# Linear attention and a gated MLP on one core: both heads of a pair of the recurrent state kept at the same columns

## The chip, the core and the metric

The kernel runs on one core of a Trainium2 chip. TensorE (PE) multiplies matrices, with its weight loads shown apart (PEld); VectorE (DVE), ScalarE (ACT) and GpSimd (POOL) work on elements; SyncE (SP) issues the DMAs. The metric is device microseconds of the whole program: 383.01 us before, the median of 3 runs (381.41 to 386.15).

## What is computed

Four batches, eight heads, 768 steps and 48 dimensions a head. Each head carries a 48 x 48 state that decays by a gate per dimension and takes up an outer product at each step; the output of a step is the query times the state:

```python
f = 1.0 / (1.0 + np.exp(-f_logit))
for t in range(S):
    state = f[:, :, t, :, None] * state + np.einsum('bhd,bhe->bhde', k[:, :, t], v[:, :, t])
    y[:, :, t] = np.einsum('bhd,bhde->bhe', q[:, :, t], state)
```

The heads side by side make x of 4 x 768 x 384. The second part is `h = relu(x @ w_in)` with 1024 columns, a 3-tap convolution of h along the sequence with a sigmoid behind it as a gate, and `(h * gate) @ w_out` back to 384 columns.

## The kernel before

The sequence of each batch is cut into 6 chunks of 128 steps; with 4 batches that makes 24 chunks, n = 0 to 23, with c the chunk's place in its batch. For each chunk:

- `stage_a` sums the logarithms of the gates along the chunk by a triangular matrix product (pl, L195), takes two exponentials of the sums (fi and fd, ScalarE) and scales the keys by fi (kp, L212) and the queries by fd (qp, L213, mostly on POOL). The decay over the whole chunk, one number per head and dimension, is put into `ft_all`, for the early chunks by small products, for the later ones by a DMA through DRAM.
- `stage_b` transposes keys and queries, two heads at a time: head j of pair p comes to partitions 64 j to 64 j + 47 (HP is 64, D is 48). The 16 partitions behind each head are zero, since the input's heads are padded to 64.
- `scores` makes 8 products of 48 x 128 by 48 x 128 (pa, L253), two halves of the array high, head j = 0 and head j = 1 into two banks of PSUM. VectorE masks them into am (L255).
- `state` makes 8 products keys by values (pk, L266) and updates the state (L273, or L276 and L277). The last chunk of a batch has no update.
- `values` makes the output in one bank, py: the state times the queries (L288, left out for the first chunk of a batch, except for the very first chunk, where the state is zero), and on top of it the masked scores times the values (L291). ScalarE rounds it into xT (L299) and VectorE stores the rest (L300); DMAs then bring together the parts of xT.

The state lies in two buffers st of 128 partitions, used in turn. For a pair of heads it is block diagonal: head 0 has partitions 0 to 47 and columns 0 to 47, head 1 partitions 64 to 111 and columns 64 to 111, and the rest was set to zero once. So one product of the whole array, 128 rows and 112 columns, serves both heads. The update goes head by head, since the columns differ: an add into tmp and a multiply by the decay, twice, with one buffer of tmp.

The MLP follows by half batches of 384 steps: `mm1` (ph, L328) with 9 products for each of 8 column blocks, each number split in two parts, then the convolution on ScalarE and VectorE (L333, L339, L340) and the gate (L342, L343); `mm2` splits the result (L358, L359) and makes the output (po, L365). The weights are split in two on ScalarE and VectorE during the first third of the program (tiles ms, L97 to L109).

The order is first set by a list: each piece of work has a due time in chunks (its chunk's number plus an offset), and the pieces are written in the order of these times. The framework's scheduler then arranges the instructions of all engines anew by its own estimate of durations and by which buffers are free. Each engine runs its instructions in its order. PSUM tiles pl, pt, pk share three buffers.

Of the kernel before, what the change touches and what calls it, by code (L numbers as in the profile page):

```python
# [9 lines left out]
F32 = mybir.dt.float32  # L10
# [5 lines left out]
ALU = mybir.AluOpType  # L16
PSUM = bass.MemoryType.PSUM
P = 128
# [4 lines left out]
CFG = dict(groups=[3, 3, 3, 3, 3, 3, 3, 3], sg=3, f1=2.6, g1=2.6, gv=2, gl=5.2, g=3.9, l=3.2, a=1.8, b=0.8, s=0.2, v=0.5, wil=(-2.3, -1.1), wis=(-0.7, 0.9), cw=1.3, wol=(1.3, 1.0), wos=2.1, wo=0.35, m1=0.5, m1s=0.9, m2=1.5, m2s=1.2, ek=(12, 24), ec='d', er='p', tp=0, tf=2, nw=2, gd=0, q0=2, lf=3, kpool=2, eg='d', eq='p', es='d', em='d', ew='p', xb=3, nf=6, fe='a', kb=4, qb=3, vb=4, lv=2.2, cb=1, sb=3, fi=1)  # L23

@with_exitstack
def gla_moe_kernel(ctx, tc, q_in, k_in, v_in, f_in, w_in, conv_w, w_out, out):


    nc = tc.nc
    B, S, H, D = v_in.shape  # L30
# [3 lines left out]
    NP = H // 2  # L34
# [9 lines left out]
    HP = 64  # L44
# [7 lines left out]
    wk = fast.enter_context(tc.tile_pool(name="wk", bufs=2))  # L52
# [17 lines left out]
    def zeroed(shape, n, name, eng):  # L70
        ts = [wk.tile(shape, F32, name=f"{name}{i}", bufs=1) for i in range(n)]
        for t in ts:
            eng.memset(t, 0.0)
        return ts
# [1 line left out]
    kp_b = [wk.tile([P, H, HP], F32, name=f"kp{i}", bufs=1) for i in range(CFG["kb"])]  # L76
    qp_b = [wk.tile([P, H, HP], F32, name=f"qp{i}", bufs=1) for i in range(CFG["qb"])]
    a_b = zeroed([P, 2, NP, P], 2, "am", nc.vector)
    s_b = zeroed([P, NP, HP + D], 2, "st", nc.vector)
    h_b = const.tile([P, NF, HS + 3], F32, name="hb")  # L80
    nc.gpsimd.memset(h_b[:, :, HS + 2:], 0.0)

    ft_all = const.tile([P, B, NC, NP], F32, name="ft_all")
# [173 lines left out]
    def state(n):  # L257
        b, c = steps[n]
        if c == NC - 1:
            return  # L260
        kp, kT, qT = tts[n]
        vt = qkv[n]
        pk = ps.tile([P, NP, D], F32, tag="s", name=f"pk{n}", bufs=3)
        for p in range(NP):
            for j in range(2):
                nc.tensor.matmul(pk[HP * j:HP * j + D, p, :], kp[:, 2 * p + j, :D], vt[:, 2 * p + j, :],  # L266
                                 start=True, stop=True)
        for j in range(2):
            r = slice(HP * j, HP * j + D)
            ft = ft_all[r, b, c, :].rearrange("p (n o) -> p n o", o=1).broadcast_to([D, NP, D])  # L270
            new = s_b[(n + 1) % 2][r, :, HP * j:HP * j + D]
            if c == 0:
                nc.vector.tensor_tensor(new, pk[r], ft, ALU.mult)  # L273
            else:
                tmp = wk.tile([P, NP, D], F32, tag="stmp", name=f"stmp{n}_{j}", bufs=1)
                nc.vector.tensor_tensor(tmp[r], pk[r], s_b[n % 2][r, :, HP * j:HP * j + D], ALU.add)  # L276
                (nc.vector if CFG["es"] == "d" else nc.gpsimd).tensor_tensor(new, tmp[r], ft, ALU.mult)  # L277

    def values(n):
        b, c = steps[n]  # L280
        kp, kT, qT = tts.pop(n)
        vt = qkv.pop(n)
        am = a_b[n % 2]
        py = ps.tile([P, NP, P], F32, tag="Y", name=f"py{n}")
        inter = c > 0 or n == 0
        if inter:
            for p in range(NP):
                nc.tensor.matmul(py[:HP + D, p, :], s_b[n % 2][:, p, :], qT[:, p, :], start=(p == 0), stop=False)  # L288
        for p in range(NP):
            for j in range(2):  # L290
                nc.tensor.matmul(py[HP * j:HP * j + D, p, :], vt[:, 2 * p + j, :], am[:, j, p, :],  # L291
                                 start=not inter and p == 0, stop=(p == NP - 1))
        hf = c // CPH
        if c % CPH == 0:
            xts[b, hf] = wk.tile([P, NP, 2, HS], F32R, tag="xT", name=f"xT{b}_{hf}", bufs=CFG["xb"])
        xT = xts[b, hf]
        ts = slice((c % CPH) * P, (c % CPH + 1) * P)
        for r in [slice(0, HP + D)] if c > 0 or n == 0 else [slice(0, D), slice(HP, HP + D)]:
            nc.scalar.copy(xT[r, :, 0, ts], py[r])  # L299
            nc.vector.tensor_tensor(xT[r, :, 1, ts], py[r], xT[r, :, 0, ts].bitcast(F32), ALU.subtract)  # L300
        if c % CPH == CPH - 1:
            for t in range(KT):
                for j in range(2):
                    s0, d0 = HP * j + GAP * t, HP * j + D
                    nc.sync.dma_start(xT[d0:d0 + GAP, t, :, :].bitcast(F32), xT[s0:s0 + GAP, KT, :, :].bitcast(F32))
# [89 lines left out]
    for n in range(N):  # L395
        plan(n - CFG["l"], lambda n=n: load_kq(n))
        plan(n - CFG["lv"], lambda n=n: load_v(n))
        plan(n - CFG["a"], lambda n=n: stage_a(n))
        plan(n - CFG["b"], lambda n=n: stage_b(n))
        plan(n - CFG["b"], lambda n=n: decay_out(n))  # L400
        plan(n - CFG["b"] + 0.4, lambda n=n: decay_in(n))
        plan(n, lambda n=n: scores(n))
        plan(n + CFG["s"], lambda n=n: state(n))
        plan(n + CFG["v"], lambda n=n: values(n))
# [29 lines left out]
    with tc.If(n_ok < P * n_ft):  # L434
        with ExitStack() as slow:
            wk = slow.enter_context(tc.tile_pool(name="swk", bufs=2))
# [11 lines left out]
            st = wk.tile([P, DG, D], F32, name="sst", bufs=1)  # L448
            nc.gpsimd.memset(st, 0.0)
            for t0 in range(0, S, TB):  # L450
# [31 lines left out]
                for t in range(0, TB, 8):  # L482
                    py = ps.tile([B * H, 8, D], F32, tag="sy", name=f"spy{t0}_{t}", bufs=2)
# [14 lines left out]
            for u in range(2 * B):  # L498
                b, hf = u // 2, u % 2
# [59 lines left out]
```

## Time and profile before

| | |
|---|---|
| median of 3 runs | 383.01 us (381.41 to 386.15) |
| the profiled execution | 384.77 us |
| its span, first to last instruction | 383.1 us |
| mean granted TensorE clock | 0.978 |
| busy: PE, PEld, DVE | 351.2, 313.2, 294.4 us |
| busy: ACT, POOL | 239.9, 60.1 us |
| chain that ended last, by engine | PE 60%, DVE 13%, ACT 9%, issue 5%, DMA 5%, POOL 3% |

A row of a group gives the line, engine, operation, output and inputs, shapes and count; behind the bar stand its busy time in us and the mean of one in ns, and then the idle time of the engine ahead of it. Matmuls are pipelined, so the mean of one is longer than the distance between two starts; the timeline, whose columns are the start in us, the length in us and the group, shows the distances. A row of a stretch gives its bounds and length in us, the busy time of each engine with the count of instructions, the granted clock, the DMA share and GB/s. A piece of the chain of waits gives its start and length in us, and engine, tile and line.

### The profile page before, as it was taken

What the parts mean: (1) busy time and instruction counts of PE and PEld (TensorE: products, weight loads), DVE (VectorE), ACT (ScalarE), POOL (GpSimd) and SP (SyncE); (2) the same over time, 40 slices, a digit from 0 to 9 for tenths busy, and PEclk for the clock granted to TensorE, in tenths of its full rate; (3) what the DMA queues carried; (4) which work ended last, traced back from release to release, by engine and by line L of the source; (5) the groups of instructions that cost most, each with busy time, mean ns of one, the idle gap of its engine ahead of it and who ended that gap; (6) DMA issues with size and microseconds to landing.
All of it is one profiled execution on the core that took longest, in us unless ns stands there. A gap on an engine that the chain in (4) does not pass through costs nothing.

```text
span 383.1 us, 7239 instructions
## 1 busy us (share of the span) xinstructions
PE 351.2 (92%) x2735; PEld 313.2 (82%) x2735; DVE 294.4 (77%) x467; ACT 239.9 (63%) x426; POOL 60.1 (16%) x72
## 2 busy tenths in 40 slices
PE   5578799868989699999999999999999999999993
PEld 1557578746978599989989999999989899999993
DVE  3999999988989968667688896669869776575620
ACT  3687669993997376645875665547545555566530
POOL 1111134311103701104011121204101100000000
PEclk9989999996999989999999999999999999999998
DMA  7999253324334330132313332232201000201011
GB/s 224 347 366 362 83 164 105 89 59 104 105 76 108 75 114 21 50 90 87 113 56 99 75 81 83 69 87 74 66 22 34 21 2 21 54 21 43 21 44 49
DMA packets 28854, 36.04 MB, mean 94 GB/s; under 512 B 10847, under 2 KB 20106, under 8 KB 28810
## 3 DMA queue, kind: packets, MB, share of 16 engines
q1 hardware_dynamic: 28810, 35.49, 31.0%
q8 instruction: 24, 0.39, 0.4%
q14 instruction: 20, 0.16, 0.2%
HBM read 28.37 MB, written 4.75 MB: 86 GB/s over the span
## 4 chain that ended last, share of the span: by engine, by line
PE 60%; DVE 13%; ACT 9%; issue 5%; DMA 5%; POOL 3%; SPq 2%; ACTq 0%; POOLq 0%; DVEq 0%
PE po L365 23%; PE ph L328 21%; PE pa L253 4%; PE py L291 4%; DMA fb<-in_f_logit_dram 4%; PE py L288 3%; POOL cgl L175 3%; PE ptk L235 2%; PE ptq L235 1%; PE pl L195 1%; ACT fb L169 1%; DVE g L340 1%; PE pk L266 1%; ACT g L342 1%; DVE am L255 1%
## 5 line engine op out<-in xcount | busy, mean ns | idle before, releaser
L328 PE MATMUL ph<-xT,wi 128*128 128x384 f32 x576 | 116.4, 349 | 4.8 <-ACT hb L331 2.7
L328 PEld LDWEIGHTS ph<-xT,wi 128*128 128x128 f32 x576 | 100.0, 189 | 10.4 <-issue 3.9
L365 PE MATMUL po<-wo,gh 128*128 128x384 f32 x384 | 101.3, 345 | 0.0
L365 PEld LDWEIGHTS po<-wo,gh 128*128 128x128 f32 x384 | 69.9, 191 | 1.2 <-issue 0.7
L365 PE MATMUL po<-wo,gl 128*128 128x384 f32 x192 | 65.8, 343 | 1.3 <-DVE gl L359 1.3
L339 DVE SCALAR_TENSOR_TENSOR g<-hb,cw,g 128x384 f32<-128x384 f32 (+1 forms) x64 | 41.0, 640 | 15.5 <-ACT g L333 15.1
L359 DVE TENSOR_TENSOR gl<-g,gh 128x1024 fp32r<-128x1024 f32 (+4 forms) x34 | 31.4, 934 | 27.1 <-ACT gh L358 27.0
L331 ACT ACTIVATE hb<-ph 128x384 f32<-128x384 f32 x64 | 31.3, 489 | 31.3 <-PE ph L328 31.2
L213 POOL TENSOR_TENSOR qp<-qp,fd 128x384 f32<-128x384 f32 x22 | 31.5, 1430 | 99.4 <-ACT fd L200 95.0
L340 DVE SCALAR_TENSOR_TENSOR g<-hb,cw,g 128x384 f32<-128x384 f32 (+1 forms) x64 | 44.2, 690 | 1.9
L343 DVE SCALAR_TENSOR_TENSOR g<-g,hb 128x768 f32<-128x768 f32 (+1 forms) x32 | 31.4, 981 | 14.6 <-ACT g L342 14.3
L342 ACT ACTIVATE g<-g 128x768 f32<-128x768 f32 (+1 forms) x32 | 27.1, 848 | 24.3 <-DVE g L340 24.3
L358 ACT CAST gh<-g 128x1024 fp32r<-128x1024 f32 (+4 forms) x34 | 26.5, 800 | 23.7 <-PE po L365 20.6
L333 ACT ACTIVATE g<-hb,cw 128x384 f32<-128x384 f32 (+1 forms) x64 | 39.6, 618 | 2.0
L365 PEld LDWEIGHTS po<-wo,gl 128*128 128x128 f32 x192 | 36.6, 191 | 1.7 <-DVE gl L359 1.5
L253 PE MATMUL pa<-qT,kT 48*128 48x128 f32 x384 | 32.8, 298 | 1.2 <-ACT qT L237 1.1
L253 PEld LDWEIGHTS pa<-qT,kT 48*128 48x128 f32 x384 | 26.1, 195 | 9.5 <-issue 5.5
L255 DVE COPY_PREDICATED am<-mask,pa 128x1024 f32<-128x1024 uint8 x24 | 31.4, 1309 | 1.2 <-PE pa L253 1.1
L291 PE MATMUL py<-am,v 128*48 128x128 f32 x384 | 27.4, 284 | 1.1 <-DVE am L255 0.9
L288 PE MATMUL py<-qT,st 128*112 128x128 f32 x168 | 24.1, 283 | 2.6 <-DVE xT L300 1.6
L291 PEld LDWEIGHTS py<-am,v 128*48 128x48 f32 x384 | 20.6, 126 | 6.1 <-DVE am L255 2.0
L299 ACT CAST xT<-py 112x512 fp32r<-112x512 f32 (+1 forms) x27 | 15.8, 585 | 15.0 <-PE py L291 11.6
(92 smaller groups left out, 428.5 us busy)
## 6 DMA issues: line engine op xcount, KB each, us to landing
kp<-in_k_dram SPq DMA_DIRECT2D x24, 256.0 KB
qp<-in_q_dram SPq DMA_DIRECT2D x24, 256.0 KB
fb<-in_f_logit_dram SPq DMA_DIRECT2D x24, 192.0 KB
v<-in_v_dram SPq DMA_DIRECT2D x24, 192.0 KB
out_dram<-ob SPq DMA_DIRECT2D x24, 192.0 KB
wis<-in_moe_w_in_dram SPq DMA_DIRECT2D x6, 512.0 KB
wos<-in_moe_w_out_dram SPq DMA_DIRECT2D x8, 384.0 KB
xT<-xT SPq DMA_DIRECT2D x48, 48.0 KB
```

Source lines behind the costliest of these rows:

```text
L213: (nc.vector if CFG["eq"] == "d" or n < CFG["q0"] else nc.gpsimd).tensor_tensor(qp[:, :, :D], qp[:, :, :D], fd, ALU.mult)
L253: nc.tensor.matmul(pa[:, j, p, :], kT[r, p, :], qT[r, p, :], start=True, stop=True)
L255: nc.vector.copy_predicated(am, mask, pa)
L288: nc.tensor.matmul(py[:HP + D, p, :], s_b[n % 2][:, p, :], qT[:, p, :], start=(p == 0), stop=False)
L291: nc.tensor.matmul(py[HP * j:HP * j + D, p, :], vt[:, 2 * p + j, :], am[:, j, p, :], start=not inter and p == 0, stop=(p == NP - 1))
L328: nc.tensor.matmul(ph, wi[:, t, wl, f * P:(f + 1) * P], xts[b, hf][:, t, xl, :], start=(i == 0), stop=(i == 3 * KT - 1))
L333: nc.scalar.activation(cv, hb[:, 1:n + 1], AF.Copy, scale=cw[:, 1, f:f + 1])
L339: nc.vector.scalar_tensor_tensor(cv, hb[:, 2:n + 2], cw[:, 2, f:f + 1], cv, ALU.mult, ALU.add)
L340: nc.vector.scalar_tensor_tensor(cv, hb[:, 0:n], cw[:, 0, f:f + 1], cv, ALU.mult, ALU.add)
L343: nc.vector.scalar_tensor_tensor(cv, cv, 1.0, h_b[:, fp:fp + 2, 1:n + 1], ALU.add, ALU.mult)
L359: nc.vector.tensor_tensor(lo, g[:, f:f + k], hi.bitcast(F32), ALU.subtract)
L365: nc.tensor.matmul(po, g[:, f, :], wo[:, f, wl, :], start=(i == 0), stop=(i == 3 * NF - 1))
```

## The change

The state is kept compactly: both heads of a pair at columns 0 to 47, head 0 on partitions 0 to 47, head 1 on 64 to 111, with 16 zero columns behind. The keys by values products are taken 64 wide, with the zero padding, so that pk is filled on all 128 partitions. Then the update is one add and one multiply over 128 partitions, with two buffers of tmp. The product of the state with the queries can no longer be one of the whole array, since the heads share columns; it becomes two of a quarter of the array each, rows and columns 0 to 63 for head 0, rows 64 to 127 and columns 64 to 111 for head 1. Nothing else is edited.

```diff
-    s_b = zeroed([P, NP, HP + D], 2, "st", nc.vector)
+    s_b = zeroed([P, NP, HP], 2, "st", nc.vector)
...
-                nc.tensor.matmul(pk[HP * j:HP * j + D, p, :], kp[:, 2 * p + j, :D], vt[:, 2 * p + j, :],
+                nc.tensor.matmul(pk[HP * j:HP * (j + 1), p, :], kp[:, 2 * p + j, :], vt[:, 2 * p + j, :],
                                  start=True, stop=True)
-        for j in range(2):
-            r = slice(HP * j, HP * j + D)
-            ft = ft_all[r, b, c, :].rearrange("p (n o) -> p n o", o=1).broadcast_to([D, NP, D])
-            new = s_b[(n + 1) % 2][r, :, HP * j:HP * j + D]
-            if c == 0:
-                nc.vector.tensor_tensor(new, pk[r], ft, ALU.mult)
-            else:
-                tmp = wk.tile([P, NP, D], F32, tag="stmp", name=f"stmp{n}_{j}", bufs=1)
-                nc.vector.tensor_tensor(tmp[r], pk[r], s_b[n % 2][r, :, HP * j:HP * j + D], ALU.add)
-                (nc.vector if CFG["es"] == "d" else nc.gpsimd).tensor_tensor(new, tmp[r], ft, ALU.mult)
+        ft = ft_all[:, b, c, :].rearrange("p (n o) -> p n o", o=1).broadcast_to([P, NP, D])
+        new = s_b[(n + 1) % 2][:, :, :D]
+        if c == 0:
+            nc.vector.tensor_tensor(new, pk, ft, ALU.mult)
+        else:
+            tmp = wk.tile([P, NP, D], F32, tag="stmp", name=f"stmp{n}", bufs=2)
+            nc.vector.tensor_tensor(tmp, pk, s_b[n % 2][:, :, :D], ALU.add)
+            nc.vector.tensor_tensor(new, tmp, ft, ALU.mult)
...
-                nc.tensor.matmul(py[:HP + D, p, :], s_b[n % 2][:, p, :], qT[:, p, :], start=(p == 0), stop=False)
+                for j in range(2):
+                    m = HP if j == 0 else D
+                    r = slice(HP * j, HP * j + D)
+                    nc.tensor.matmul(py[HP * j:HP * j + m, p, :], s_b[n % 2][r, p, :m], qT[r, p, :],
+                                     start=(p == 0), stop=False)
```

The scheduler makes a new order of all engines from this. On VectorE, before, the update of chunk 2 (pk_459 the keys by values, stmp_0 and stmp_1 the two heads' tmp, mswi and mscw the splitting of weights):

```order
L276 TENSOR_TENSOR stmp_0_468<-pk_459,st_95 48x192
L255 COPY_PREDICATED am_91<-mask_82,pa_438 128x1024
L98 TENSOR_SCALAR mscw<-mscw 24x128
L103 SCALAR_TENSOR_TENSOR mswi_1_338<-wis_148,mswi_1_338 128x512
L108 TENSOR_TENSOR mswi_1_338<-mswi_1_338,wi 128x512
L277 TENSOR_TENSOR st_96<-stmp_0_468,ft_all 48x4x48
L99 TENSOR_SCALAR mscw<-mscw 24x128
L109 TENSOR_TENSOR wi<-mswi_1_338 128x512
L276 TENSOR_TENSOR stmp_1_471<-pk_459,st_95 48x192
L300 TENSOR_TENSOR xT_0_294<-py_520,xT_0_294 112x4x128
L101 SCALAR_TENSOR_TENSOR mscw<-cws,mscw 24x128
L277 TENSOR_TENSOR st_96<-stmp_1_471,ft_all 48x4x48
```

After, the same update on VectorE (pk_463; the lines below the edit have other numbers, L302 is L300 of before):

```order
L274 TENSOR_TENSOR stmp_472<-pk_463,st_95 128x192
L212 TENSOR_TENSOR kp_87<-kp_87,fi_381 128x8x48
L109 TENSOR_TENSOR wi<-mswi_1_341 128x512
L302 TENSOR_TENSOR xT_0_297<-py_419,xT_0_297 112x4x128
L275 TENSOR_TENSOR st_96<-stmp_472,ft_all 128x4x48
```

Twelve places, four of them of the update, have become five with two of the update; the masking of this chunk's scores (L255) now stands behind the update instead of inside it.

On TensorE, before, around the state product of chunk 14 (py_2159; ptq the transposed queries, ph the MLP):

```order
L235 MATMUL ptk_2134<-ident,kp_87 128x128 x4
L235 MATMUL ptq_2141<-ident,qp_88 128x128 x4
L288 MATMUL py_2159<-qT_1974,st_95 112x128 x4
L291 MATMUL py_2159<-am_91,v_1768 48x128 x8
L328 MATMUL ph_6_2181<-xT_1_1429,wi 128x384 x5
```

After, the same chunk on TensorE (py_2174; L289 is the state product, L293 the values):

```order
L235 MATMUL ptq_2156<-ident,qp_88 128x128 x4
L289 MATMUL py_2174<-qT_1988,st_95 64x128
L289 MATMUL py_2174<-qT_1988,st_95 48x128
L289 MATMUL py_2174<-qT_1988,st_95 64x128
L289 MATMUL py_2174<-qT_1988,st_95 48x128
L289 MATMUL py_2174<-qT_1988,st_95 64x128
L289 MATMUL py_2174<-qT_1988,st_95 48x128
L289 MATMUL py_2174<-qT_1988,st_95 64x128
L289 MATMUL py_2174<-qT_1988,st_95 48x128
L293 MATMUL py_2174<-am_91,v_1786 48x128 x3
L195 MATMUL pl_2165<-cgh_1665,tri 128x384
```

Four products of 112 columns have become eight of 64 and 48 in turn, and the values of this chunk now have a gate sum in their midst. Over the whole order the pieces of consecutive state products are 30 instead of 26, since some are broken in the same way.

## The prediction

> **What bounds the kernel now.** I read the busy times of the whole execution first, then the engines by stretch, then the chain of waits.
>
> ```profile
> PE 351.2 (92%) x2735; PEld 313.2 (82%) x2735; DVE 294.4 (77%) x467; ACT 239.9 (63%) x426; POOL 60.1 (16%) x72
> ...
> 20.00:70.00 50.00, 43.61 (x447) 34.14 (x447) 49.32 (x95) 39.52 (x86) 13.63 (x7) 0.97 0.65 212
> 70.00:90.00 20.00, 13.50 (x116) 10.54 (x114) 18.86 (x35) 15.79 (x27) 4.87 (x6) 0.91 0.24 62
> 90.00:150.00 60.00, 55.34 (x434) 48.74 (x433) 51.86 (x85) 45.68 (x76) 12.77 (x11) 0.94 0.32 89
> 150.00:360.00 210.00, 209.81 (x1595) 195.58 (x1595) 157.49 (x228) 123.35 (x210) 26.03 (x33) 1.00 0.21 57
> ```
>
> The columns behind each stretch are its length, then PE, PEld, DVE, ACT and POOL busy. There are two regimes. From 20 to 70 us VectorE is busy 49.32 of 50 us and TensorE only 43.61. From 150 to 360 us TensorE is busy 209.81 of 210 and VectorE 157.49. So VectorE time counts early, and after 150 us only TensorE time does. Between 20 and 150 us TensorE idles 130 - 112.45 = 17.6 us: the most that a relief of other engines can give there. The chain agrees; its pieces include these:
>
> ```profile
> 37.93 1.05 DVE st L277
> ...
> 46.22 1.06 DVE st L277
> ...
> 52.96 4.08 DMA fb<-in_f_logit_dram
> ...
> 61.70 4.52 POOL cgl L175
> ...
> 84.53 3.45 DMA xT<-xT
> ...
> 116.11 1.08 DVE st L277
> ...
> 117.33 1.10 PE py L288 x8
> ```
>
> Three state multiplies are links of it, the last one shortly ahead of a state product; between 52 and 88 us its long links are a gate load, a POOL run and the xT copies.
>
> **VectorE: 72 instructions become 36.** Of 24 chunks 20 update the state; 4 of them (a batch's first) take 2 multiplies, 16 take 2 adds and 2 multiplies. After the change it is 1, or 1 and 1.
>
> ```profile
> L277 DVE TENSOR_TENSOR st<-stmp,ft_all 48x192 f32<-48x192 f32 x32 | 13.3, 415 | 0.6
> L276 DVE TENSOR_TENSOR stmp<-pk,st 48x192 f32<-48x192 f32 x32 | 11.2, 352 | 0.6
> ...
> L273 DVE TENSOR_TENSOR st<-pk,ft_all 48x192 f32<-48x192 f32 x8 | 2.8, 350 | 0.1
> ...
> L300 DVE TENSOR_TENSOR xT<-py,xT 112x512 fp32r<-112x512 f32 x21 | 14.4, 687 | 0.9 <-ACT xT L299 0.4
> ...
> L300 DVE TENSOR_TENSOR xT<-py,xT 48x512 fp32r<-48x512 f32 x6 | 4.1, 686 | 1.4 <-ACT xT L299 1.4
> ```
>
> No row has 128x192. The two forms of L300 answer that: 112 partitions take 687 ns, 48 take 686, so the number of partitions costs nothing, and I take 352 ns for each new add and multiply. Removed are 16 x 0.352 + 16 x 0.415 + 4 x 0.350 = 13.7 us. Where they lie:
>
> ```profile
> 20.00:70.00 50.00, 6.97 (x16) 0.97 0.65 212
> ...
> 90.00:150.00 60.00, 6.31 (x16) 0.94 0.32 89
> 150.00:360.00 210.00, 11.25 (x32) 1.00 0.21 57
> ```
>
> These are the adds and multiplies with tmp; the first-chunk multiplies stand apart:
>
> ```profile
> 20.00:70.00 50.00, 0.70 (x2) 0.97 0.65 212
> 70.00:90.00 20.00, 0.71 (x2) 0.91 0.24 62
> ```
>
> Half of 11.25 goes after 150 us, where TensorE hides it: worth nothing. Before that, half of 6.97, 6.31, 0.70 and 0.71 makes 7.3 us: the most that can reach the end, with 0 as the least.
>
> How much reaches the end? The multiplies of 1.05 us in the chain, three times the usual, stood beside POOL. Two of the cases:
>
> ```profile
> 37.63 1.13 POOL L213 TENSOR_TENSOR qp<-qp,fd 128x384 f32<-128x384 f32 x1 [6.24 <-ACT fd L200]
> 46.06 1.01 POOL L213 TENSOR_TENSOR qp<-qp,fd 128x384 f32<-128x384 f32 x1 [7.30 <-ACT fd L200]
> ```
>
> The multiply at 37.93 ends at 38.98, where POOL ends at 38.76; 46.22 ends at 47.28, POOL at 47.07. So a state multiply can wait out a POOL one; with half as many there will be fewer such hits. In 20 to 52 us lie one first-chunk update and three others, together 0.35 + 3 x 0.70 = 2.5 us saved, 3.9 if both long multiplies go as well (two times 0.7 more): I take 3.2. From 52 to 88 us the chain hangs on the load, POOL and the copies above, and I take nothing. From 88 to 150 us four updates save 2.8 to 3.5 us in a chain that they share with other work; I take 1.0, for the link at 116.11. VectorE gives -4.2 us (from 0 to -7.3).
>
> The state's path is shorter too. It was add, multiply, add, multiply with other work between, for chunk 1 from the row below to the end of the multiply at 37.93, 5.3 us; now it is one of each:
>
> ```profile
> 33.69 0.34 DVE L276 TENSOR_TENSOR stmp<-pk,st 48x192 f32<-48x192 f32 x1
> ```
>
> What waited for it, by the view of waits (us, times, longest):
>
> ```profile
> PE py L288 <- DVE st L277: 0.9, 2, 0.7
> ```
>
> 0.9 us in two waits; I leave them to the favourable end. The second tmp buffer is worth nothing (0.6 us idle ahead of all adds), nor are the smaller memsets, which stand at the program's start.
>
> **TensorE: 4 state products a chunk become 8 of a quarter array each.** 21 chunks have it.
>
> ```profile
> L288 PE MATMUL py<-qT,st 128*112 128x128 f32 x168 | 24.1, 283 | 2.6 <-DVE xT L300 1.6 <-DVE st L277 0.9
> ```
>
> A float32 product is two instructions (168 = 21 x 4 x 2), so 16 a chunk replace 8. The nearest rows are the other two tiled products, each 16 a chunk: scores in half-height tiles (L253), values in half-width tiles (L291).
>
> ```profile
> 244.67 1.04 PE L288 MATMUL py<-qT,st 128*112 128x128 f32 x8
> 245.63 1.08 PE L291 MATMUL py<-am,v 128*48 128x128 f32 x16
> 246.65 1.85 PE L328 MATMUL ph<-xT,wi 128*128 128x384 f32 x9
> 248.42 0.49 PE L253 MATMUL pa<-qT,kT 48*128 48x128 f32 x4
> 248.84 1.85 PE L328 MATMUL ph<-xT,wi 128*128 128x384 f32 x9
> 250.63 0.94 PE L253 MATMUL pa<-qT,kT 48*128 48x128 f32 x12
> 251.50 0.56 PE L266 MATMUL pk<-v,kp 128*48 128x48 f32 x16
> 251.99 0.65 PE L235 MATMUL ptk<-ident,kp 128*128 128x128 f32 x4
> ...
> 260.33 1.16 PE L253 MATMUL pa<-qT,kT 48*128 48x128 f32 x16
> 261.42 0.38 PE L266 MATMUL pk<-v,kp 128*48 128x48 f32 x8
> ```
>
> From start to next start, the 8 full products take 245.63 - 244.67 = 0.96 us, 16 values 1.02, 16 scores 1.09. So both kinds of half tile run in overlapping pairs, at twice the rate per instruction. If quarter tiles do so too, 16 cost between 1.02 and 1.09: +0.06 to +0.13 a chunk, 1.3 to 2.7 us over 21. Scores are the nearer row, since they too have 48 rows: +2.3, rounded down for the smaller weight load (48 or 64 columns, not 128). Breaking a group costs: 4 scores from 248.42 and 12 from 250.63 took 0.42 + 0.87 = 1.29 us against 1.09 for 16 in one piece, so 0.2 a break. The new order has 30 pieces of state product for 26, and a few more of values and scores, fewer of updates: I add 0.7. Update products load 64 columns, not 48; the 16 at 251.50 take 0.49, their loads hidden: 0, at most 0.1 a chunk, 2 us. TensorE costs +3.0 us (from 1.3 to 5).
>
> A gain on TensorE is excluded: at best both tiles of a pair run in the time of one full product.
>
> **Sum.** 3.0 - 4.2 = -1.2 us on the profiled 384.77 us (span 383.1), 383.6; that execution lies 1.8 above the median of 383.01, so 381.8, said as 382. The ends: -7.3 - 0.9 + 1.3 = -6.9, or 376, and +5, or 388.
>
> **Rivals.** *No overlap.* All diagonal tiles write one bank of py, and scores write two banks, one for each half. If the two quarter tiles cannot run at once, 16 instructions take the full tile's time each, 1.92 us a chunk for 0.96: 20 us over 21 chunks, of which these lie where nothing hides them:
>
> ```profile
> 150.00:360.00 210.00, 11.80 (x88) 10.98 (x88) 1.00 0.21 57
> ```
>
> 88 of the 168 instructions are 11 chunks, 10.6 us; so +10 to +20, 393 to 403. It decides once a chunk's product passes 0.96 + 7.7 / 21 = 1.33 us. For it: no row shows two row tiles in one bank. Against it: values put two column tiles in one bank (L291) and overlap, and the two halves here share no partition either. The Trainium skill, "TensorEngine Tiling (Array Packing)", Restrictions and Gotchas, says that different row tiles cannot access the same PSUM bank at the same time; by that rule this rival holds, and no run here shows it yet. 0.13.
>
> *Early relief in full.* All 7.3 us pass on, with the 0.9 us of waits and up to 1.0 us more (the excess of the long multiplies, 6.97 + 6.31 - 32 x 0.35 = 2.1 us, of which half is counted already), and quarter tiles are no slower than full ones: -8.2 to -9.2, 374 to 375. For it: VectorE at 99% there. Against: from 52 to 88 us the chain hangs on loads. 0.10.
>
> *The order slips.* The scheduler rebuilt the whole order. One gate piece put later costs a POOL run of this size on the chain:
>
> ```profile
> 123.67 6.25 POOL L175 TENSOR_TENSOR cgl<-fb,cgh 128x1152 fp32r<-128x1152 f32 x1 [1.32 <-ACT cgh L174]
> ```
>
> One or two such runs with part of the forecast gain lost are +5 to +10, 388 to 393. 0.10. That 128 partitions cost more than 48 is spoken against by L300.
>
> **How the numbers follow.** Forecast 382, its own range 376 to 388, 0.67. A difference of 2%, 7.7 us, is about what a measurement can tell. Faster by more is early relief, 0.10; slower by more is no overlap and half of the slip, 0.13 + 0.05 = 0.18; the rest, 0.72, is within 2%. The range 374.5 to 393 leaves out no overlap and the far half of early relief, 0.18.
>
> **What would show it.** State updates: 36 VectorE instructions near 0.35 us, VectorE near 281 us. State products: 336 instructions, 16 a chunk from start to next start in 1.0 to 1.1 us, with starts 0.06 apart; 0.1 apart, or 1.9 a chunk, is no overlap. TensorE still full from 150 us on, which may begin 2 to 5 us earlier. Wrong it would be if the new adds took well over 0.35 us, or TensorE's idle time before 150 us grew.

## The result, and the profile after

The changed kernel takes 387.0 us in the median of 20 runs (383.97 to 389.24), the kernel before 384.46 us beside it (20 runs, 381.41 to 387.53). The ratio is 1.0062, with a 95% interval of 1.004 to 1.0084: 2.4 us slower. That is within 2%, and within the range, but the sum had said 1.2 us faster.

First the busy times and the stretches of the profiled execution after (its own time 387.15 us, span 385.3); columns as before:

```profile
PE 360.5 (94%) x2903; PEld 315.3 (82%) x2903; DVE 282.2 (73%) x431; ACT 240.2 (62%) x426; POOL 51.6 (13%) x72
...
20.00:70.00 50.00, 46.48 (x472) 35.62 (x470) 46.38 (x86) 36.70 (x81) 10.09 (x7) 0.87 0.63 203
70.00:90.00 20.00, 13.29 (x116) 10.66 (x113) 17.73 (x33) 19.65 (x35) 1.72 (x3) 0.94 0.22 62
90.00:150.00 60.00, 60.00 (x492) 51.90 (x491) 50.97 (x79) 45.68 (x75) 11.08 (x13) 0.96 0.34 94
150.00:360.00 210.00, 210.00 (x1667) 191.13 (x1666) 148.89 (x205) 121.36 (x206) 25.89 (x33) 1.00 0.21 57
```

VectorE fell from 294.4 to 282.2 us. TensorE's idle time between 20 and 150 us fell from 17.6 to 130 - 119.8 = 10.2 us, and from 90 us on it is full. But its busy time rose by 9.3 us. The state's groups on VectorE:

```profile
L274 DVE TENSOR_TENSOR stmp<-pk,st 128x192 f32<-128x192 f32 x16 | 5.6, 351 | 2.5 <-PE pk L266 2.2
L275 DVE TENSOR_TENSOR st<-stmp,ft_all 128x192 f32<-128x192 f32 x16 | 5.6, 349 | 0.1
L271 DVE TENSOR_TENSOR st<-pk,ft_all 128x192 f32<-128x192 f32 x4 | 1.4, 349 | 0.0
```

36 instructions of 0.35 us, and none of them long: exactly what was costed. TensorE around the state product that stood at 244.67 us before, and one that is broken by a gate sum:

```profile
227.58 0.65 PE L289 MATMUL py<-qT,st 48*64 48x128 f32 x8
228.16 0.45 PE L195 MATMUL pl<-cgh,tri 128*128 128x384 f32 x1
228.44 0.34 PE L195 MATMUL pl<-cgl,tri 128*128 128x384 f32 x1
228.71 0.65 PE L289 MATMUL py<-qT,st 48*64 48x128 f32 x8
229.28 1.08 PE L293 MATMUL py<-am,v 128*48 128x128 f32 x16
...
244.46 1.09 PE L289 MATMUL py<-qT,st 48*64 48x128 f32 x16
245.47 1.08 PE L293 MATMUL py<-am,v 128*48 128x128 f32 x16
...
251.55 0.67 PE L266 MATMUL pk<-v,kp 128*64 128x48 f32 x16
252.16 0.66 PE L235 MATMUL ptk<-ident,kp 128*128 128x128 f32 x4
...
257.08 0.34 PE L195 MATMUL pl<-cgh,tri 128*128 128x384 f32 x1
257.25 0.34 PE L195 MATMUL pl<-cgl,tri 128*128 128x384 f32 x1
257.43 0.34 PE L367 MATMUL po<-wo,gl 128*128 128x384 f32 x1
```

Unbroken, the 16 quarter products take 1.01 us, 0.063 from start to start on average: the pairs overlap. Broken, they take 0.58 + 0.57 = 1.15, and the gate sum between the pieces 0.28 + 0.27, where one between output products, at 257.08, takes 0.17 + 0.18. The update products take 0.60 us, where they took 0.50 (the rows' starts are rounded, and give 0.61 and 0.49).

The groups from 150 us to the end, before:

```profile
L288 PE MATMUL py<-qT,st 128*112 128x128 f32 x88 | 11.8, 273 | 0.0
...
L266 PE MATMUL pk<-v,kp 128*48 128x48 f32 x160 | 6.7, 214 | 0.0
```

and after:

```profile
L289 PE MATMUL py<-qT,st 48*48 48x128 f32 (+1 forms) x176 | 13.2, 277 | 0.0
...
L266 PE MATMUL pk<-v,kp 128*64 128x48 f32 x160 | 7.9, 229 | 0.0
```

For the same number of chunks the state product has 1.4 us more and the update products 1.2. These are prices in a stretch where nothing hides them.

The two timelines can be laid side by side from the scores of chunk 13 to the last output product, with the same work between. Before:

```profile
178.34 1.16 PE L253 MATMUL pa<-qT,kT 48*128 48x128 f32 x16
...
376.82 0.34 PE L365 MATMUL po<-wo,gl 128*128 128x384 f32 x1
```

and after:

```profile
176.36 1.16 PE L253 MATMUL pa<-qT,kT 48*128 48x128 f32 x16
...
379.18 0.34 PE L367 MATMUL po<-wo,gl 128*128 128x384 f32 x1
```

The changed kernel comes to the first row 2.0 us earlier, and from there it takes 202.8 us instead of 198.5, 4.3 more: a gain early and a larger loss late.

### The profile page after: what moved, and what is told of

Same layout as the page of the kernel before. It is cut to its first block, busy times and chain, and to the rows that moved or that the text cites. A ratio compares the mean times of both kernels' runs of the same rounds, so it can differ in the third digit from the quotient of the medians.

```text
span 385.3 us, 7519 instructions
## 1 busy us (share of the span) xinstructions
PE 360.5 (94%) x2903; PEld 315.3 (82%) x2903; DVE 282.2 (73%) x431; ACT 240.2 (62%) x426; POOL 51.6 (13%) x72
## 4 chain that ended last, share of the span: by engine, by line
PE 78%; ACT 9%; DMA 4%; DVE 4%; SPq 1%; issue 1%; ACTq 0%; DVEq 0%
PE po L367 27%; PE ph L330 25%; PE pa L253 6%; PE py L293 6%; PE py L289 5%; PE pk L266 3%; PE ptk L235 3%; PE pl L195 2%; PE ptq L235 2%; DMA wis<-in_moe_w_in_dram 2%; ACT fb L169 1%; DMA fb<-in_f_logit_dram 1%; ACT g L335 1%; ACT fb L170 1%; DMA qp<-in_q_dram 1%
## 5 line engine op out<-in xcount | busy, mean ns | idle before, releaser
L367 PE MATMUL po<-wo,gh 128*128 128x384 f32 x384 | 100.1, 342 | 0.0
L341 DVE SCALAR_TENSOR_TENSOR g<-hb,cw,g 128x384 f32<-128x384 f32 (+1 forms) x64 | 39.7, 623 | 21.6 <-ACT g L335 21.5
L342 DVE SCALAR_TENSOR_TENSOR g<-hb,cw,g 128x384 f32<-128x384 f32 (+1 forms) x64 | 44.4, 695 | 1.9
L213 POOL TENSOR_TENSOR qp<-qp,fd 128x384 f32<-128x384 f32 x22 | 27.9, 1270 | 99.7 <-ACT fd L200 93.7
L253 PE MATMUL pa<-qT,kT 48*128 48x128 f32 x384 | 34.7, 304 | 1.6 <-ACT qT L237 1.6
L253 PEld LDWEIGHTS pa<-qT,kT 48*128 48x128 f32 x384 | 27.7, 201 | 9.9 <-issue 6.9
L255 DVE COPY_PREDICATED am<-mask,pa 128x1024 f32<-128x1024 uint8 x24 | 31.4, 1308 | 1.5 <-PE pa L253 1.5
L212 DVE TENSOR_TENSOR kp<-kp,fi 128x384 f32<-128x384 f32 x22 | 25.3, 1149 | 7.5 <-ACT fi L199 7.5
L293 PE MATMUL py<-am,v 128*48 128x128 f32 x384 | 30.1, 292 | 0.0
L289 PE MATMUL py<-qT,st 48*48 48x128 f32 (+1 forms) x336 | 27.5, 291 | 0.1
L293 PEld LDWEIGHTS py<-am,v 128*48 128x48 f32 x384 | 22.5, 130 | 5.8 <-issue 4.1
```

Source lines behind the costliest of these rows:

```text
L253: nc.tensor.matmul(pa[:, j, p, :], kT[r, p, :], qT[r, p, :], start=True, stop=True)
L255: nc.vector.copy_predicated(am, mask, pa)
L289: nc.tensor.matmul(py[HP * j:HP * j + m, p, :], s_b[n % 2][r, p, :m], qT[r, p, :], start=(p == 0), stop=False)
L341: nc.vector.scalar_tensor_tensor(cv, hb[:, 2:n + 2], cw[:, 2, f:f + 1], cv, ALU.mult, ALU.add)
L342: nc.vector.scalar_tensor_tensor(cv, hb[:, 0:n], cw[:, 0, f:f + 1], cv, ALU.mult, ALU.add)
L367: nc.tensor.matmul(po, g[:, f, :], wo[:, f, wl, :], start=(i == 0), stop=(i == 3 * NF - 1))
```

## Experiments

The theories that the expectations name: A, TensorE pays the prices just read, and VectorE's relief gives part of them back; B, the scheduler's new order decides; C and D, the price or the relief never reaches the end. All ratios are to the kernel before, run beside them.

**One part at a time, all chunks.** Two parts of the change, its relief without its price, and a second tmp buffer alone.

```diff
 e1: the state product alone, state block diagonal
-    py[:HP + D, p, :], s_b[n % 2][:, p, :], qT[:, p, :]
+    for j: py[HP * j:HP * j + m, p, :], s_b[n % 2][r, p, HP * j:HP * j + m], qT[r, p, :]
 e2: the update products alone
-    pk[HP * j:HP * j + D, p, :], kp[:, 2 * p + j, :D]
+    pk[HP * j:HP * (j + 1), p, :], kp[:, 2 * p + j, :]
 e3: one head's update
-    for j in range(2):
+    for j in range(1):
 e4: two buffers of tmp
-    name=f"stmp{n}_{j}", bufs=1
+    name=f"stmp{n}_{j}", bufs=2
```

> The kernel before with only its state product split into two quarter-array products a pair; the state stays block diagonal, the update stays two adds and two multiplies. Theory A (TensorE pays): in the profile after, 16 quarter products take 1.01 us with 0.1 us more ahead of them for the change of tile, against 0.96, so 0.05 to 0.15 us a chunk; 11 chunks lie in the full stretch and 10 in the early one, so +1.6 to +3.2 us, ratio 1.004 to 1.008. Theory B (the new order decides): no relation to that sum, between -3 and +3 us. Theory C (the loss is from elsewhere): 0, ratio 1.000.

> The kernel before with only the keys by values products taken 64 wide instead of 48. Theory A (TensorE pays): after the change 16 of them take 0.60 us against 0.49, so 0.11 us a chunk in 20 chunks; +1.1 us (the chunks of the full stretch alone) to +2.2 us, ratio 1.003 to 1.006, with 0.60 us for 16 in this profile too. The prediction's own term was 0. Theory B (order): its order differs little from before, so 0.

> The kernel before with the update of the second head of each pair left out (its state stays zero, so the odd heads miss what came from earlier chunks): VectorE has 36 state instructions fewer, as after the change, and TensorE the same products as before. Theory A: the early relief arrives, -2 to -4.2 us, ratio 0.989 to 0.995. Theory D (the relief never reaches the end, since loads and POOL hold the early stretch): 0, ratio 0.998 to 1.002. If A, TensorE's idle time before 150 us falls by as much.

> The kernel before with two buffers of tmp and nothing else: a small change of the order with no work added or removed. Theory A: within 1 us of before, ratio 0.998 to 1.002. Theory B (the order alone moves the time by as much as was measured): 2 us or more either way.

Measured: e1 0.997 (0.9944 to 0.9995), e2 0.9974 (0.9946 to 1.0002), e3 1.0103 (1.0052 to 1.0154), e4 1.0153 (1.011 to 1.0196). All four miss theory A: the prices came out as small gains (e2's interval reaches 1), the relief as a loss, and a change that adds and removes no work cost 1.5%, 5.9 us. The stretches of e4 show where:

```profile
20.00:70.00 50.00, 41.77 (x446) 32.87 (x444) 46.39 (x86) 35.27 (x80) 9.69 (x7) 0.97 0.64 212
70.00:90.00 20.00, 15.68 (x112) 13.81 (x112) 17.16 (x32) 18.70 (x31) 3.72 (x3) 0.83 0.21 53
90.00:150.00 60.00, 51.93 (x440) 46.84 (x439) 54.95 (x91) 43.67 (x72) 12.32 (x12) 0.91 0.35 98
150.00:360.00 210.00, 209.76 (x1571) 193.91 (x1567) 158.91 (x226) 123.27 (x212) 25.85 (x34) 1.00 0.20 56
```

Between 20 and 150 us TensorE idles 130 - 109.4 = 20.6 us, 3 more than before, with the same work; in the full stretch TensorE is as busy as before. So an edit that touches the first chunks gets a new early order, and that alone can be worth several microseconds. Edits of all chunks cannot be told apart in this way.

**The same order for all.** With the scheduler's estimate of durations off, the order follows the list of due times, and the parts differ little in it.

```diff
 e5 to e8: before, and with the edit of e2, of e1, of the whole change
-    TileContext(nc, schedule_with_timeline_sim=True)
+    TileContext(nc, schedule_with_timeline_sim=False)
```

> The kernel before, unchanged but for the scheduler's setting: it arranges the instructions without its estimate of durations, so that the order follows the list of due times much closer. It is the base of the next three, whose orders then hardly differ from it (pieces of work on TensorE in other places: 0, 8 and 42 of 1028; with the estimate they were 118 for the changed kernel). No theory gives its time: slower than before by any amount, for lack of the rearranging.

> The base without the estimate, with the keys by values products 64 wide instead of 48; its order is the base's exactly. Theory A (the loads of 64 columns are paid): 0.11 us a chunk, against the base +1.1 to +2.2 us. Theory C (hidden behind other waits): 0, within 1 us.

> The base without the estimate, with the state product in two quarter-array products a pair and the block diagonal state kept; nearly the base's order. Theory A: 0.05 to 0.15 us a chunk where TensorE is full, against the base +1.6 to +3.2 us. Theory C: 0, within 1 us.

> The changed kernel without the estimate, so with nearly the order of the base. Theory A (prices as in the profile, relief as forecast): the two prices of 2.7 to 5.4 us less a relief of 4.2 us, -1.5 to +1.2 us against the base. Theory D (no relief): +2.7 to +5.4 us. Theory B (the slower result came from the new order alone): against the base at or below 0, where the changed kernel with the estimate was +2.4 us.

Measured: e5 1.03 (1.0247 to 1.0353), e6 1.0285 (1.0236 to 1.0335), e7 1.0546 (1.0491 to 1.06), e8 1.0263 (1.0211 to 1.0315). The whole change is level with its base, as theory A's middle; the quarter products alone cost 2.5%, three times what A gave at most; the wide loads cost nothing that shows (the interval leaves 0.7% either way). In this order TensorE is not full to the row from 150 us on (e5: 205.33 of 210 us to 360), so a price can hide. e7 was left unexplained here. The parts do not add up in this order: e8 has e7's products too and is 2.8% below it, which is more than the relief alone gives further down (e14, 1.2%).

**The late half alone.** The early order stays what it was if only chunks 12 to 23 are edited: the order is made forward, and up to those chunks it is the one of before row for row. What they change falls into TensorE's full stretch.

```diff
 e9: the whole change; e10: the state product; e11: the update products; each
+    if n >= 12:
 e12: the whole change
+    if n < 12:
```

> The whole change, but only for chunks 12 to 23 (state kept compactly from the third batch on, with its own two buffers of tmp); chunks 0 to 11 stay as before, and the order up to them is the one of before to the row. So only the full stretch of TensorE is changed. Theory A (TensorE's prices are paid there): 10 products at 0.13 us and 10 updates at 0.11 us more, by the distances of starts in the profile after, with some broken groups: +2 to +3.5 us, ratio 1.005 to 1.009. The prediction's own terms gave +1.1 to +2.0 there. Theory B (it was the early order alone): 0, ratio 0.998 to 1.002.

> The kernel before with quarter-array state products for chunks 12 to 23 alone, block diagonal state kept, order before them as it was. Theory A: 10 times 0.13 us, +0.5 to +2 us, ratio 1.001 to 1.005. Theory B: 0.

> The kernel before with 64-wide keys by values products for chunks 12 to 23 alone, order before them as it was. Theory A: 10 times 0.11 us, +0.5 to +1.5 us, ratio 1.001 to 1.004. The prediction's term was 0 (loads hidden); theory B too.

> The whole change, but only for chunks 0 to 11 (later chunks as before; the second head's old compact columns are left in the buffers, so later odd-half products take up stale numbers). The order changes from the first chunk on. Theory A (relief less price): 11 products and 10 updates cost 2.5 us at most where TensorE idles anyway, the relief is 4.2 us or less: -2 to +0.5 us. Theory B (the new early order decides): anything from -4 to +5 us; together with the late half it should make up the whole change's +2.4 us.

Measured: e9 1.0147 (1.0109 to 1.0186), that is +5.6 us; e10 1.0086 (1.0047 to 1.0125), +3.3; e11 1.0049 (1.0022 to 1.0077), +1.9. The parts add up to the whole, 1.35% for 1.47%, with some 0.6% of uncertainty between them: VectorE's relief is worth nothing that shows there, as the prediction said, and each part costs something. e12, the first half alone, took 0.9898 (0.9861 to 0.9935), -3.9 us; up to 167 us its TensorE order is that of the changed kernel, row for row. The two halves make -1.0 + 1.5 = +0.5%, for 0.6% measured: this is the result, taken apart. Not all of e12's gain is relief: from the scores of chunk 13 to the last output product its profile takes 374.84 - 177.64 = 197.2 us, 1.3 less than before with the same products, by the order alone. The size of e9 is above theory A's 2 to 3.5 us. Its stretches:

```profile
90.00:150.00 60.00, 55.30 (x431) 49.29 (x426) 52.65 (x88) 45.93 (x77) 13.85 (x12) 0.94 0.33 92
150.00:360.00 210.00, 210.00 (x1650) 191.39 (x1649) 149.06 (x204) 121.87 (x207) 25.50 (x33) 1.00 0.21 57
```

From 90 to 150 us TensorE's busy time is that of before to 0.1 us (55.34), and it is full from there: the loss is TensorE work. Which work, the two timelines say from the first state product behind 150 us on, a row at the same place of both orders. The last row before is the output product at 376.82, shown above; the first is

```profile
156.85 1.03 PE L288 MATMUL py<-qT,st 128*112 128x128 f32 x8
```

and in e9 the two are

```profile
155.44 1.03 PE L300 MATMUL py<-qT,st 128*112 128x128 f32 x8
...
379.87 0.34 PE L383 MATMUL po<-wo,gl 128*128 128x384 f32 x1
```

That is 219.97 us before and 224.43 in e9, 4.5 us more, with the same chunks between. Added up from the start of each row to the start of the next: the state products take 1.5 us more, the update products 1.1 (0.11 for each of ten chunks), the gate sums 0.6, the query transposes 0.5, the low output products 0.4, the values 0.3, the rest nothing on balance. So 2.6 us are the two products themselves, and 1.8 stand in rows whose instructions the change does not touch. They lengthen where tiles of another size follow: a query transpose takes 0.44 us to the start of a state product before, and in e9

```profile
202.05 0.60 PE L235 MATMUL ptq<-ident,qp 128*128 128x128 f32 x4
202.58 1.08 PE L305 MATMUL py<-qT,st 48*64 48x128 f32 x16
```

0.53; three gate sums that stand between products of parts of the array take 0.55 instead of 0.35; and a low output product takes 0.27 before such a product instead of 0.18, in more places than before. So a change of tile costs some 0.09 us here, and the new order has more of them. The values' 0.3 us are one more broken group.

The profiles of e10 and e11 show less than their medians. Over the same stretch they take 222.3 and 220.3 us, 2.3 and 0.3 more than before. In e10 0.8 us of that is one wait of TensorE for ScalarE (at 195.34); in e11 the update products take 1.2 us more and the scores 0.7 less, in a somewhat other order. The rest of the two medians is not shown by their profiles; executions with one and the same early order come to the first row anywhere from 154.16 us (e10) to 156.85 (before), so one profile of a kernel does not settle a microsecond. How e9's price divides between the two products is therefore known by the distances in its own profile, and only roughly by the runs.

**What was open.** The relief alone in the plain order (e3's edit), the late state product alone in it (e10's edit), the changed kernel with narrower loads, and the early half made whole.

```diff
 e16: second head 48 wide, update over 112 partitions
-    pk[HP * j:HP * (j + 1), p, :], kp[:, 2 * p + j, :]
+    pk[HP * j:HP * j + m, p, :], kp[:, 2 * p + j, :m]      # m = HP if j == 0 else D
 e13, e17: e12, and before the block diagonal chunks
+    for t in s_b: nc.gpsimd.memset(t[HP:, :, :D], 0.0)
 e18: e17 with the edit of e16
```

> The base without the scheduler's estimate, with the second head's update left out (odd heads miss what came from earlier chunks): VectorE's relief alone, with no price on TensorE and nearly the base's order. Theory A (relief is real): -3 to -8 us against the base without the estimate (396 us, 1.030 of before), so 1.010 to 1.022 of before. Theory D (no relief, the early half's gain is luck of the order): 1.027 to 1.033.

> The base without the estimate, with quarter-array state products for chunks 12 to 23 alone; order the base's. Theory A (0.13 us a chunk and some broken groups): +1.3 to +3.3 us against the base's 1.030 of before, so 1.033 to 1.039; the other 5 us of all quarter products in the plain order then lie in the early half. If the whole 8 us are late: 1.05.

> The changed kernel with the second head's keys by values products 48 wide again and the update over 112 partitions instead of 128, which the state products do not notice. Half of the load price of 0.11 us a chunk goes: 16 products in 0.54 to 0.55 us instead of 0.60. Theory A: 0.6 to 1.2 us faster than the changed kernel, 1.003 to 1.005 of before, unless its new early order outweighs that, by up to 4 us either way as seen.

> The whole change for chunks 0 to 11, later chunks as before, and two small memsets on POOL at the end of the second batch that clear the second head's compact columns, so that the later block diagonal chunks start from zeros. Its order is that of the early half before. Expected by its run: 0.990 of before (0.986 to 0.994), so about 3.5 us faster than before and 6 us faster than the changed kernel. If the memsets wait in a bad place, 1 us less.

> The whole change for chunks 0 to 11, later chunks as before; the second head's compact columns are cleared by two memsets on POOL at chunk 12, behind the last compact product. Order as in the early half. Theory A (relief early, no price late): 0.990 of before (0.986 to 0.994), about 3.5 us faster than before. If the order alone had made the early half's gain, the same time, since the order is the same; so this run settles the version, not the cause.

> The same with the second head's keys by values products 48 wide and the update over 112 partitions. Theory A: 10 chunks at 0.05 us, where TensorE idles in part, so 0 to 0.5 us faster than the run before it, 0.986 to 0.994 of before; the order differs in some twenty places on TensorE, which can move it by more.

e14 took 1.0179 (1.0137 to 1.0221), 1.2% below the base's 1.03, with intervals apart: in the plain order leaving out these VectorE instructions is worth 4.6 us. TensorE's idle time between 20 and 150 us falls from 26.5 to 20.6 us with it. The order is only nearly the base's, though (on TensorE some 36 of 628 rows stand elsewhere, on VectorE more), so a share of this may be the order's. e15 took 1.0376 (1.0343 to 1.0409), 0.8% or 2.9 us above the base, though the two intervals touch: the late price, as in e10. So of e7's 2.5% some 1.7% lie in the early half, and that was not traced further.

e15 and its base have the same TensorE order to two places, so their timelines can be laid side by side from 152 us on. To the last output product e5 takes 367.46 - 152.16 = 215.30 us, e15 370.42 - 152.53 = 217.89, 2.6 us more, and 2.1 of them are in the state products. Where these stand in one piece they take 1.01 us for 0.97. Four of the ten edited chunks have a gate sum in the midst of them, and those cost 0.4 to 0.5 us more each; two of the four are broken in e5 too, 6 + 2, and there it costs e5 nothing (0.58 + 0.31, for 0.97 in one piece). In e15 the same place takes 0.80 + 0.57. The rows of that case, e5:

```profile
194.13 0.82 PE L288 MATMUL py<-qT,st 128*112 128x128 f32 x6
194.71 0.45 PE L195 MATMUL pl<-cgh,tri 128*128 128x384 f32 x1
194.99 0.34 PE L195 MATMUL pl<-cgl,tri 128*128 128x384 f32 x1
195.16 0.38 PE L288 MATMUL py<-qT,st 128*112 128x128 f32 x2
195.47 0.42 PE L291 MATMUL py<-am,v 128*48 128x128 f32 x2
```

and e15:

```profile
194.60 0.87 PE L294 MATMUL py<-qT,st 48*64 48x128 f32 x10
195.40 0.44 PE L195 MATMUL pl<-cgh,tri 128*128 128x384 f32 x1
195.68 0.34 PE L195 MATMUL pl<-cgl,tri 128*128 128x384 f32 x1
195.94 0.63 PE L294 MATMUL py<-qT,st 48*48 48x128 f32 x6
196.51 0.42 PE L298 MATMUL py<-am,v 128*48 128x128 f32 x2
```

The two full instructions behind the sum take 0.31 us; the six quarter ones take 0.57, and the 10 ahead of it 0.80 for 0.58. Where a break falls matters: a pair of heads is four of these instructions, and 10 + 6 or 6 + 10 split a pair and take 1.36 us in all, in e9 as in e15, where 8 + 8 and 4 + 12 fall between pairs and take 1.15.

e16 took 0.9975 (0.995 to 1.0), 0.9% below the changed kernel, where theory A had 0.2 to 0.3% for the loads. The loads did not give even that. The 16 update products, 64 and 48 columns in turn, still take 0.60 us, not the 0.54 to 0.55 expected, since the half of the array with 64 columns keeps its pace:

```profile
248.76 0.67 PE L267 MATMUL pk<-v,kp 128*64 128x48 f32 x16
249.36 0.66 PE L235 MATMUL ptk<-ident,kp 128*128 128x128 f32 x4
```

From the scores of chunk 13 to the last output product e16 takes 376.30 - 173.40 = 202.9 us, as the changed kernel does. Its gain is all ahead of that, where its order differs in some places; that the order makes it is likely, but was not tried apart. e13 took 0.9916 (0.9885 to 0.9947); its memsets stood ahead of chunk 11's output, whose second heads thus missed their state. e17 has them behind it: 0.9906 (0.9877 to 0.9936), 380.94 us for 384.59. e18 took 0.9871 (0.9834 to 0.9908), 378.92 us: the fastest version here, faster than both kernels. Against e17 it gains early too: it comes to the scores of chunk 13 at 173.27 us, e17 at 176.91, and takes 197.0 us from there, e17 197.1. Its stretches:

```profile
20.00:70.00 50.00, 46.83 (x472) 35.54 (x472) 45.74 (x89) 39.24 (x85) 8.99 (x7) 0.93 0.63 202
70.00:90.00 20.00, 15.43 (x138) 12.01 (x139) 18.99 (x34) 17.85 (x32) 3.79 (x4) 0.89 0.21 58
90.00:150.00 60.00, 60.00 (x494) 52.75 (x492) 51.52 (x76) 47.11 (x77) 10.31 (x15) 0.98 0.33 92
150.00:360.00 210.00, 210.00 (x1614) 196.62 (x1611) 156.81 (x227) 123.41 (x210) 26.69 (x33) 1.00 0.21 57
```

TensorE idles 7.7 us between 20 and 150 us (17.6 before, 10.2 after), and late it runs full products: 1614 instructions where the changed kernel has 1667.

## Why the prediction was right or wrong

- *Two regimes, VectorE early, TensorE late*: right. The late half's relief gained nothing that shows (e9 is no better than e10 and e11 together), the early one was worth something (e14; e12 with the order's share in it).
- *VectorE, 13.7 us less, 0.35 us for 128 partitions*: right. The state's rows fell from 27.3 to 12.6 us with means of 349 to 351 ns, and VectorE as a whole from 294.4 to 282.2. That there would be fewer long multiplies beside POOL: none is left among these 36. But standing beside POOL is not enough to make one long: the multiply at 54.65 us stands inside a POOL run from 54.50 to 56.62 and took 0.34, and it is the POOL run that is twice as long as others of its kind.
- *Relief of 4.2 us at the end*: of that size in the plain order (4.6 us, e14, with what its order changed). For the changed kernel itself it cannot be told from the order: e12 gained 3.9 us (2.5 to 5.3) net of its own price, about what the forecast has for that half, but 1.3 of that stand in the late stretch of its profile; and e1 and e2, which relieve nothing, also gained early, if the late prices of 0.9 and 0.5% are in them, since they end 0.3% below before. That the size agrees may be luck.
- *TensorE +3.0 us*: this is the step that failed, by its size. By its own rates the ten late chunks should have cost 1.1 us (0.11 each) to 2.0 (0.13 each and all 0.7 for the breaks); the whole change there cost 5.6 (4.2 to 7.1), 4.5 of them in the one profiled pair, and in the changed kernel itself 4.3 from chunk 13 on. With the first half at -3.9 this turns the sum from a gain into a loss. The state product was right: 1.01 us in one piece, said 1.0 to 1.1, and 1.5 us over the ten chunks with its breaks. What was put at nothing makes the rest. The loads of 64 columns were taken as hidden, with 2 us over all chunks as the bound; the update products cost 0.11 us a chunk by the distances, 1.1 of the 4.5 us, and 1.9 us (0.8 to 3.0) by the runs of e11. The 16 products that were read as hiding their loads were no evidence of it, since no row showed a stream in which the loads do not count. Rows that the change leaves alone hold the other 1.8 us, most of it in changes of tile. Breaks were put at 0.2 us each and four more of them over the whole order; of the ten late chunks four are broken in e9 (two before), and a break costs from 0.14 us (8 + 8, at 227.58) to 0.35 (10 + 6, e15), with 0.2 more in a gate sum between. How much of the 1.1 us between the profiled pair and the runs of e9 is real is open.
- *No overlap, 393 to 403*: it did not come, as its 0.13 had it. The starts are 0.063 us apart on average, with both row tiles in one bank of py. The Trainium skill's rule ("TensorEngine Tiling (Array Packing)", Restrictions and Gotchas), that different row tiles cannot access the same bank at the same time, does not hold for these two, which share no partition; no run here tries two that do.
- *The order slips, +5 to +10 us, 0.10*: as a kind it was real and its chance too low. e4, with no work changed, lost 1.5%. The net of the changed kernel's own order is not known.
- *A difference of 2% is about what a measurement can tell*: too wide here; 20 runs of each kernel told 0.6% (0.4 to 0.84). That 387 lies inside the stated range is owed to its upper end of +5 us; the way of the change was forecast wrong.

## What to carry to other kernels

A saving on one engine and a price on another are to be summed stretch by stretch, and the price in the stretch where its engine is full counts whole: here the same edit gained 1% in the first half of the program and lost 1.5% in the second, and doing it in the first half alone beat both kernels. Under a scheduler that rebuilds the order, a small edit can carry a change of order that weighs more than the edit (5.9 us in e4, where no work changed); a control that changes no work shows how much, and an edit of the later chunks alone keeps the order ahead of them. A price per instruction should be read from groups as they will stand, broken ones too, and with the rows beside them.

## What was not expected of the hardware

Weight loads of 64 columns instead of 48 lengthen a stream of 16 half-array products with 48 moving columns from 0.50 to 0.60 us, although they run beside the products. In the traces the products of one half of the array start every 45 ns with 48 columns and every 58 with 64, each some 43 ns behind its own load in both, which speaks for the loads as what sets the distance; no run parts loads and products. In e16 the two paces stand side by side: from 248.76 us on the narrow half's products start every 45 ns and are through 0.09 us earlier, and the wide half, at 58, sets the 0.60 us.

TensorE's granted clock in the early stretch differs between the two profiled executions. In tenths, over 40 slices of the span, before and then after:

```profile
PEclk9989999996999989999999999999999999999998
```

```profile
PEclk9585999996999999999999999999999999999999
```

After, the second and the fourth slice are at half. The scores in the fourth, with the row behind them:

```profile
29.93 2.08 PE L253 MATMUL pa<-qT,kT 48*128 48x128 f32 x16 [0.81 <-ACT qT L237]
31.94 1.09 PE L266 MATMUL pk<-v,kp 128*64 128x48 f32 x16
```

The 16 scores take 2.01 us to the next start, and the update products 1.02, for 0.60 at full clock. Over the 20 runs of the changed kernel the mean clock went from 0.946 to 0.993, with no relation to the time (384.53 us at 0.957, 389.24 at 0.99); over those of the kernel before, the slower ones tend to the lower clock. What sets it here was not tried.
